# Chunks of 64 steps on 64x64 array tiles in a recurrent attention block followed by routed experts

## The chip, the cores and the metric

The kernel runs on one core of one Trainium2 chip. The metric is the device time of one launch in microseconds (us). Five engines work in the core, each through its own instructions in order: TensorE (PE in the profile, with its weight loads listed apart as PEld), VectorE (DVE), ScalarE (ACT), GpSimd (POOL) and SyncE (SP, which here only issues DMAs). Products land in PSUM, which here is eight banks of 128 partitions by 512 floats; everything else lies in SBUF.

## What is computed

A recurrent attention with a matrix state per batch and head, then a top-1 mixture of experts over its output. All values are 32-bit floats.

```python
# attention: B, H, S, D = 4, 8, 768, 40
for t in range(S):
    y[:, :, t] = einsum('bhd,bhde->bhe', r_t, state)
    Sa = einsum('bhde,bhe->bhd', state, a_t)
    state_decay = state * w_t[:, :, None, :] - einsum('bhd,bhe->bhde', Sa, b_t)
    state = state_decay + einsum('bhd,bhe->bhde', v_t, k_t)
# x = y as (3072 rows, 320), then experts: E = 8, F = 1024
logits = x @ w_gate;  e = argmax(logits);  gate = softmax(logits)[e]
out = gate * (relu(x @ w1[e]) @ w2[e])
```

## The kernel before

**Chunks.** The time axis is cut into 6 chunks of 128 steps. A unit is one chunk of one batch with all 8 heads, and there are 24 units (`u`; chunk `c`, batch `b`). Two heads share the partitions: head parity `par` 0 uses partitions 0 to 39, parity 1 uses 64 to 103 (`rows(par)`), and `NP` = 4 pairs lie side by side.

**Inside a unit.** `load` brings the six inputs in two DMAs. `prepare` forms the running product of the decay `w` (four scans, L160), its reciprocal (L161), scales `a`, `k` and `b` by them (POOL and DVE), and transposes V, K, B and the decay to time-major form on TensorE (L169), with ScalarE copies out of PSUM (L171). `systems` forms four 128x128 matrices per head, masked to a triangle (`twin`, L190 and L194): N (steps acting on later steps), its transpose NT, G and A. It then squares N and NT five times (`product`, L177, copied by ScalarE in L180). `attend` needs the solution U of a triangular system: it starts from the right-hand side (L239, L245) and multiplies with NT, NT^2, NT^4 ... NT^32 in eight dependent steps per parity (`apply`, L231, with an add on DVE after each, L255 and L264). Then come U transposed (L268), a masked product ZT, the state update (L282, L286, L294, L295), the state transposed (L302), and the output in three products (L310, L316, L320). `route` transposes the output (L335), forms the gate's logits (L339) and a softmax scale, and stores the scaled rows to DRAM (L349).

**Order.** The loop emits for each unit: load of `u + 2`, `prepare` and `systems` of `u + 1`, `attend` and `route` of `u`. The planner of the language puts the instructions of each engine into an order of its own from these, by priority of emission and by its own cost figures, and adds all waits. Units of the same batch depend on each other through the state; there are four batches, so four units lie between the uses of one state.

**After attention.** The expert weights of the first two experts are fetched, the rows are sorted by expert (one-hot products, L386 to L484), then eight expert groups of 512 rows run: gather, transpose, two layers (L513, L526), scatter to the output.

**PSUM.** Tag `big` has 5 slots of one bank (128 x 512 floats), tag `small` 3 slots. Every float product is recorded as two weight loads and two matmuls; a "pass" below is one such pair of a load and a matmul.

## Time and profile before

| | |
|---|---|
| time, median of 3 runs | 2159.66 us (2152.96 to 2162.82) |
| the profiled execution | 2158.44 us |
| its span, first to last instruction | 2156.7 us |
| TensorE busy, share of the span | 92% (weight loads 80%) |
| VectorE, ScalarE, GpSimd busy | 24%, 19%, 7% |
| mean granted TensorE clock | 0.751 of full speed |
| attention, from the first matrices to the store of the last rows | 28.4 to 1779 us |
| sorting and experts | 1779 to 2157 us |

The profile records one execution. Each instruction has an engine, a line of the code, its output and input tiles, a duration, and the idle time of its engine before it with what ended it. Matmuls are pipelined, so a busy TensorE is not one at its peak: the rate is read from the distance between starts, or from a group's length over its count. [...]

### The profile page before, as it was taken

The page shows a single profiled execution, that of the slowest core. Times are in us where ns is not written, and L with a number is a line of the kernel's source. Part 1 is how long each engine was busy: PE and PEld are TensorE (multiplying, and loading weights), DVE is VectorE, ACT ScalarE, POOL GpSimd, SP SyncE. Part 2 cuts the span into 40 slices and gives each one's busy share as a digit, 9 for nine tenths or more (in the row PEclk, how much of TensorE's full clock was granted, in tenths as well). Part 3 has the DMA queues.
Part 4 walks back from the last instruction along what each step waited for, and adds up shares of the span by engine and source line. Part 5 has one row for each costly group of instructions (what it writes and reads, how often), then busy time and mean ns, then how long its engine had stood idle before and what let it go on. Part 6 is the DMA issues. An engine that isn't in the chain of part 4 may idle for free.

```text
span 2156.7 us, 29213 instructions
## 1 busy us (share of the span) xinstructions
PE 1991.0 (92%) x12916; PEld 1728.3 (80%) x12916; DVE 518.7 (24%) x1157; ACT 417.4 (19%) x849; POOL 151.1 (7%) x185
## 2 busy tenths in 40 slices
PE   5999889999999999999999999999999985999998
PEld 4998889988988898899889888988898872554454
DVE  3312321322232133213322321341221113111110
ACT  1322122212211221122122112211222100100000
POOL 4000000000000000000000000000000003211011
PEclk9976577667856775777577667766886657999999
DMA  2000000000000000000000000000000004322210
GB/s 55 20 4 22 22 19 4 22 22 1 22 22 19 4 23 22 19 4 22 22 1 22 22 19 4 22 22 19 4 23 4 1 3 150 108 93 80 73 50 12
DMA packets 20560, 59.58 MB, mean 28 GB/s; under 512 B 2893, under 2 KB 14159, under 8 KB 18512
## 3 DMA queue, kind: packets, MB, share of 16 engines
q1 hardware_dynamic: 16992, 48.50, 7.9%
q0 software_dynamic: 3072, 9.18, 1.4%
q8 instruction: 102, 1.67, 0.3%
q14 instruction: 26, 0.21, 0.0%
q10 hardware_dynamic: 368, 0.01, 0.0%
HBM read 49.82 MB, written 9.18 MB: 27 GB/s over the span
## 4 chain that ended last, share of the span: by engine, by line
PE 65%; issue 13%; DVE 4%; POOL 2%; DMA 0%; ACT 0%; POOLq 0%; DVEq 0%
PE ps_q L231 20%; PE ps_NT L177 9%; PE ps_N L177 6%; PE ps_y L320 3%; PE ps_y L316 3%; PE ps_nat L169 3%; PE ps_y L310 3%; PE ps_ZT L190 2%; PE ps_r L245 2%; DVE X L255 2%; POOL out_dram L532 1%; PE ps_GT L190 1%; PE ps_AT L190 1%; PE ps_N L190 1%; PE hp L513 1%
## 5 line engine op out<-in xcount | busy, mean ns | idle before, releaser
L231 PE MATMUL ps_q<-X,NT 128*128 128x40 f32 x2304 | 397.1, 332 | 51.8 <-DVE X L255 51.6
L231 PEld LDWEIGHTS ps_q<-X,NT 128*128 128x128 f32 x2304 | 375.7, 247 | 69.0 <-DVE X L255 68.6
L177 PE MATMUL ps_NT<-NT,N 128*128 128x128 f32 x1920 | 285.4, 296 | 2.1 <-DVE N L194 1.0
L177 PEld LDWEIGHTS ps_NT<-NT,N 128*128 128x128 f32 x1920 | 243.7, 200 | 10.3 <-DVE N L194 3.3
L255 DVE TENSOR_TENSOR X<-ps_q,X 128x160 f32<-128x160 f32 x240 | 77.9, 324 | 635.3 <-PE ps_q L231 635.3
L180 ACT COPY NT<-ps_NT 128x512 f32<-128x512 f32 x240 | 140.7, 586 | 385.9 <-PE ps_NT L177 385.9
L177 PE MATMUL ps_N<-N,NT 128*128 128x128 f32 x1536 | 211.1, 282 | 0.0
L177 PEld LDWEIGHTS ps_N<-N,NT 128*128 128x128 f32 x1536 | 196.3, 200 | 0.0
L513 PE MATMUL hp<-xgT,w 128*128 128x512 f32 (+1 forms) x384 | 191.3, 628 | 0.0
L231 PE MATMUL ps_q<-Z,NT 128*128 128x40 f32 x768 | 141.7, 347 | 28.0 <-DVE Z L264 28.0
L231 PEld LDWEIGHTS ps_q<-Z,NT 128*128 128x128 f32 x768 | 132.2, 260 | 37.3 <-DVE Z L264 36.7
L513 PEld LDWEIGHTS hp<-xgT,w 128*128 128x128 f32 (+1 forms) x384 | 63.2, 189 | 122.8 <-issue 121.7
L526 PE MATMUL zp<-w,h_sb 128*128 128x320 f32 x512 | 145.0, 433 | 0.0
L320 PE MATMUL ps_y<-natB,ZT 128*128 128x40 f32 x384 | 119.3, 415 | 13.5 <-DVE ZT L194 13.5
L180 ACT COPY N<-ps_N 128x512 f32<-128x512 f32 x192 | 112.5, 586 | 74.3 <-PE ps_N L177 74.3
L526 PEld LDWEIGHTS zp<-w,h_sb 128*128 128x128 f32 x512 | 94.5, 191 | 34.5 <-issue 0.8
L316 PE MATMUL ps_y<-natK,AT 128*128 128x40 f32 x384 | 119.1, 414 | 0.0
L320 PEld LDWEIGHTS ps_y<-natB,ZT 128*128 128x128 f32 x384 | 102.8, 330 | 16.4 <-DVE ZT L194 15.2
L270 ACT COPY uT<-ps_uT 128x512 f32<-128x512 f32 x24 | 14.1, 586 | 486.0 <-PE ps_uT L268 486.0
L316 PEld LDWEIGHTS ps_y<-natK,AT 128*128 128x128 f32 x384 | 102.5, 328 | 2.0
L169 PE MATMUL ps_nat<-ident,in 128*128 128x128 f32 x288 | 76.0, 420 | 24.6 <-DMA in<-in_packed_dram 16.5
L158 POOL MEMSET PT<- 128x4 f32 x24 | 2.5, 106 | 1330.8 <-DVE ST L295 1047.0
(150 smaller groups left out, 1874.1 us busy)
## 6 DMA issues: line engine op xcount, KB each, us to landing
in<-in_packed_dram SPq DMA_DIRECT2D x48, 480.0 KB
w<-in_moe_w_dram SPq DMA_DIRECT2D x8, 1280.0 KB
w<-in_moe_w_dram SPq DMA_DIRECT2D x8, 1024.0 KB
x_rows<-xs SPq DMA_DIRECT2D x24, 160.0 KB
w<-in_moe_w_dram SPq DMA_DIRECT2D x8, 256.0 KB
xg<-x_rows,g_idx POOLq DMA_INDIRECT x32, 3.0
out_dram<-zo,s_idx POOLq DMA_INDIRECT x32, 2.5
wg_sb<-in_moe_w_gate_dram ACTq DMA_DIRECT2D x2, 4.0 KB
```

Of the source, the lines that this page charges most:

```text
L169: nc.tensor.transpose(ps[:, p, :], src[:, p, :], ident[:])
L177: nc.tensor.matmul(ps[:, p, :], lhsT=lhs(p), rhs=rhs(p), start=True, stop=True)
L180: nc.scalar.copy(t[:], ps[:])
L190: nc.tensor.matmul(ps[par][:, p, :], lhsT=lhs(par, p), rhs=rhs(par, p), start=True, stop=True)
L231: nc.tensor.matmul(q[:, p, :], lhsT=m[:, p, :], rhs=x[:, p, :], start=True, stop=True)
L245: nc.tensor.matmul(qr[par][:, p, :], lhsT=d["GT"][par][:, p, :], rhs=nV[:, p, par, :D], start=(c == 0 and p == 0), stop=True, skip_group_c ...
L255: nc.vector.tensor_tensor(Xn[:], q[:], X[:], op=ALU.add)
L310: nc.tensor.matmul(qy[par][:, p, :], lhsT=I[rs, R, p, :], rhs=Sn[rs, p, :], start=(p == 0), stop=False, skip_group_check=True,)
L316: nc.tensor.matmul(qy[par][:, p, :], lhsT=d["AT"][par][:, p, :], rhs=nK[:, p, par, :D], start=(c == 0 and p == 0), stop=False, skip_group_ ...
L320: nc.tensor.matmul(qy[par][:, p, :], lhsT=ZT[par][:, p, :], rhs=nB[:, p, par, :D], start=False, stop=True, skip_group_check=True,)
L513: nc.tensor.matmul(hp[:, :cols], lhsT=g["w"][0][:dsz, db, fb * 128 : (fb + 1) * 128], rhs=g["xT"][:dsz, db, :cols], start=(db == 0), stop= ...
L526: nc.tensor.matmul(zp[:], lhsT=g["h"][:, fb, j * 128 : (j + 1) * 128], rhs=g["w"][1][:, fb, :], start=(fb == 0), stop=(fb == FB - 1),)
```

## The change

A unit becomes one chunk of 64 steps of two batches (`bh`, two halves of the batch axis) with all heads: there are again 24 units, 12 chunks by 2. Batch `q` and head parity `par` each pick a half of 64 partitions, on the input or the output side, so every product but the transposes and the gate becomes a 64x64 product on one of the four quarters of the array. `TILES` lists the four quarters, and the loops issue them in that order. Where input and output half are the same index, only the two diagonal quarters are used: `ps_T1`, `ps_gv`, `ps_u`, `ps_S` and the first addition into `ps_y`.

The five squarings stay in number (the last forms one side only), but the inverse is now formed as a matrix, TT = (1+N)(1+N^2)...(1+N^32), in `systems`, with the identity added on GpSimd (`plus_one`) and each product copied by VectorE. `attend` then applies TT once, in place of eight dependent steps per parity. The decay's running product and its reciprocal become two scans over all segments at once and a reciprocal of 8 columns. The decay is no longer transposed, since the output is scaled before its transpose. PSUM has one tag of 4 slots with two banks each. `prepare` runs two units ahead and `systems` one. The weights of the first two experts are fetched before the attention loop; loads go three units ahead, with eight DMAs of 256-byte pieces each.

The diff, cut to its core:

```diff
-W, K, A, B_, V, R = range(6)
+K, A, B_, V, R = range(5)
...
+    C = 64
+    BH = B // 2
+    NCH = NW * CW // C
...
+    halves = [slice(0, HP), slice(HP, 128)]
+    TILES = [(0, 0), (1, 1), (0, 1), (1, 0)]
...
+        NIN = 4
+        ins = [ring.tile([128, 5, SEG, C], F32, name=f"in{i}") for i in range(NIN)]
+        decs = [ring.tile([128, SEG * C1 + 1], F32, name=f"dec{i}") for i in range(2)]
...
+        for t in ins:
+            for lo in (32, 96):
+                nc.gpsimd.memset(t[lo : lo + 32], 0.0)
+        for t in decs:
+            for lo in (32, 96):
+                nc.gpsimd.memset(t[lo : lo + 32], 1.0)
+            nc.gpsimd.memset(t[:, : SEG * C1].rearrange("p (s j) -> p s j", j=C1)[:, :, 0:1], 0.0)
+            nc.gpsimd.memset(t[:, SEG * C1 :], 0.0)
+        for t in qini + rhss + STs + Ss:
+            nc.gpsimd.memset(t[:], 0.0)
...
+        def bank2(name):
+            return pp.tile([128, 2, 512], F32, name=name, tag="ps")
...
+        def load(u):
+            c, bh = divmod(u, BH)
...
+            for q in range(2):
+                for par in range(2):
+                    src = packed[2 * bh + q, at, par, :, :, :, w0 : w0 + C]
+                    nc.sync.dma_start(dst[rows(par), q, :, 1:], src[:, 0])
+                    nc.sync.dma_start(dst5[rows(par), q], src[:, 1:])
+
+        def prepare(u):
...
+            nc.vector.tensor_tensor_scan(
+                rv[:, : SEG * C1 + 1][:, ::-1], dec[:, ::-1], ones65[:, ::-1], 0.0, op0=ALU.mult, op1=ALU.add,
+            )
...
+            nc.vector.reciprocal(qi[:, :, 0], r3[:, :, 1])
+            nc.vector.tensor_tensor_scan(
+                q[:], dec[:, : SEG * C1], qi[:].rearrange("p s j -> p (s j)"), 0.0, op0=ALU.mult, op1=ALU.add,
+            )
...
+            nc.gpsimd.tensor_tensor(I[:, K], I[:, K], behind, op=ALU.mult)
+            nc.gpsimd.tensor_tensor(I[:, B_], I[:, B_], behind, op=ALU.mult)
+            nc.gpsimd.tensor_tensor(I[:, A], I[:, A], d["q3"][:, :, :C], op=ALU.mult)
...
+            for i, (nm, n) in enumerate((("V", V), ("K", K), ("B", B_))):
...
+                for p in range(NP):
+                    nc.tensor.transpose(
...
+                nc.scalar.copy(t[:].rearrange("c p a d -> c (p a d)"), ps[:, i % 2, :])
+            return d
...
+        def systems(d):
...
+            ps = tens(bank2("ps_N"), 2)
+            for p in range(NP):
+                for w, (l, r) in enumerate(((A, B_), (B_, A))):
+                    for par, q in TILES:
+                        nc.tensor.matmul(
+                            ps[halves[q], par, w, p, :], lhsT=head(l, p, q, par), rhs=head(r, p, q, par), start=True, stop=True,
+                        )
+            X = sb.tile([128, 2, 2, NP, C], F32, name="X", bufs=4)
+            for s in range(2):
+                nc.vector.tensor_tensor(
+                    X[:, s], ps[:, s], m_nn[:, :, None, :].to_broadcast([128, 2, NP, C]), op=ALU.mult,
+                )
...
+            pt = bank2("ps_T1")
+            p1 = pt[:, 0, :].rearrange("x (q p j) -> x q p j", q=2, p=NP)
+            for p in range(NP):
+                for par, q in TILES:
+                    nc.tensor.matmul(
+                        p1[halves[par], q, p, :], lhsT=head(B_, p, q, par), rhs=head(A, p, q, par), start=True, stop=True,
+                    )
+            T1 = sb.tile([128, 2, NP, C], F32, name="T1", bufs=2)
+            nc.vector.tensor_tensor(T1[:], p1, m_nn[:, None, 1:2, :].to_broadcast([128, 2, NP, C]), op=ALU.mult)
...
+            def plus_one(dst, src):
+                nc.gpsimd.tensor_tensor(dst, src, eye[:, : NP, :], op=ALU.add)
+
+            for s in range(2):
+                plus_one(TT[:, s], T1[:, s])
+            ps = tens(bank2("ps_G"), 2)
...
+                nc.vector.tensor_tensor(
+                    G[:, s], ps[:, s], m_up[:, None, None, :].to_broadcast([128, 2, NP, C]), op=ALU.mult,
+                )
...
+            for p in range(NP):
+                for par, q in ((0, 0), (0, 1), (1, 0), (1, 1)):
+                    nc.tensor.matmul(
+                        gv[halves[q], par, p, :], lhsT=G[halves[q], par, 0, p, :], rhs=Vn[halves[q], p, par, :D],
+                        start=True, stop=True,
+                    )
...
+            nc.scalar.copy(GV[:, :, :, :D], gv)
...
+            k = 1
+            while k < C:
+                nk = 2 * k
+                if nk < C:
+                    last = 2 * nk >= C
+                    ps = tens(bank2("ps_sq"), 2)
+                    for p in range(NP):
+                        for w in range(1 if last else 2):
+                            for h, s in TILES:
+                                nc.tensor.matmul(
+                                    ps[halves[s], h, w, p, :], lhsT=X[halves[h], s, 1 - w, p, :], rhs=X[halves[h], s, w, p, :],
+                                    start=True, stop=True,
+                                )
+                    Y = sb.tile([128, 2, 2, NP, C], F32, name="X", bufs=4)
+                    M = sb.tile([128, 2, NP, C], F32, name="M", bufs=2)
+                    if last:
+                        nc.scalar.copy(Y[:, :, 0], ps[:, :, 0])
+                    else:
+                        for s in range(2):
+                            nc.scalar.copy(Y[:, s], ps[:, s])
+                    for s in range(2):
+                        plus_one(M[:, s], Y[:, s, 0])
+                if k > 1:
+                    ps = tens(bank2("ps_TT"), 2)
+                    for p in range(NP):
+                        for h, s in TILES:
+                            nc.tensor.matmul(
+                                ps[halves[s], h, 0, p, :], lhsT=Mk[halves[h], s, p, :], rhs=TT[halves[h], s, p, :],
+                                start=True, stop=True,
+                            )
+                    TT = sb.tile([128, 2, NP, C], F32, name="TT", bufs=3)
+                    nc.vector.tensor_copy(TT[:], ps[:, :, 0])
+                if nk < C:
+                    X, Mk = Y, M
+                k = nk
+            d["TT"] = TT
...
+        def attend(u, d):
...
+                nc.vector.tensor_tensor(ST[:, :, :, :D], state[bh][:], pc, op=ALU.mult)
...
+                for p in range(NP):
+                    for par, q in TILES:
+                        nc.tensor.matmul(
+                            ps[halves[q], par, p, :], lhsT=I[halves[par], A, 2 * p + q, :], rhs=ST[halves[par], q, p, :D],
+                            start=True, stop=True,
+                        )
+                nc.vector.tensor_tensor(rhs[:, :, :, :D], ps, rhs[:, :, :, :D], op=ALU.add)
+
+            pu = bank2("ps_u")[:, 0, : 2 * NP * D].rearrange("x (a p d) -> x a p d", a=2, p=NP)
+            for p in range(NP):
+                for par, q in ((0, 0), (0, 1), (1, 0), (1, 1)):
+                    nc.tensor.matmul(
+                        pu[halves[q], par, p, :], lhsT=TT[halves[q], par, p, :], rhs=rhs[halves[q], par, p, :D],
+                        start=True, stop=True,
+                    )
+            U = sb.tile([128, 2, NP, D], F32, name="U")
+            nc.scalar.mul(U[:], pu, -1.0)
+
...
+                nc.scalar.copy(Sn[:, :, :, :D], pS)
...
+                with tc.issue_after(first.ins):
+                    by_dims()
+            uT = sb.tile([128, 2, NP, C], F32, name="uT")
+            nc.scalar.copy(uT[:], put)
...
+            nc.vector.tensor_tensor(
+                ZT[:], pz, m_nn[:, None, 1:2, :].to_broadcast([128, 2, NP, C]), op=ALU.mult,
+            )
...
+                    nc.vector.tensor_tensor(sa[:], pst, ST[:, :, :, :D], op=ALU.add)
...
+            nc.vector.tensor_tensor(
+                xT[:].rearrange("x p q j -> x q p j"), py, q3[:, :, :C].rearrange("x (p q) j -> x q p j", q=2), op=ALU.mult,
+            )
...
+        def route(u, xT):
...
+                r0 = (2 * bh + q) * S + c * C
+                nc.sync.dma_start(x_d[r0 : r0 + C, :], xs[halves[q]].rearrange("x h e -> x (h e)"))
...
+        NU = BH * NCH
+        weights = {}
+        ready = {}
+        for u in range(min(2, NU)):
+            load(u)
+        for e in range(2):
+            weights[e] = fetch(moe_w1[e], moe_w2[e])
+        for u in range(-2, NU):
+            if u >= -1 and u + 3 < NU:
+                load(u + 3)
+            if u + 2 < NU:
+                ready[u + 2] = prepare(u + 2)
+                ready[u + 2]["u"] = u + 2
+            if 0 <= u + 1 < NU:
+                systems(ready[u + 1])
+            if u >= 0:
+                route(u, attend(u, ready.pop(u)))
+
```

Per unit the loops give 480 products on quarters of the array (32, 16, 32, 16, 4x32 + 16 and 5x16 in `systems`; 16, 16, 16, 16, 16, 16, 32 and 32 in `attend`) and 20 on the full array (12 transposes in `prepare`, 4 gate products and 4 transposes in `route`).

## Rows read from the trace of the kernel before

**Rows 1.** Page, part 1: busy time, share of the span and instructions of each engine.

```profile
PE 1991.0 (92%) x12916; PEld 1728.3 (80%) x12916; DVE 518.7 (24%) x1157; ACT 417.4 (19%) x849; POOL 151.1 (7%) x185
```

**Rows 2.** Windows by stage: length, busy us (count) of PE, PEld, DVE, ACT, POOL; clock; DMA.

```profile
0.00:28.40 28.40, 3.84 (x17) 3.14 (x17) 6.01 (x8) 3.04 (x4) 24.14 (x49) 1.00 0.40 104
28.40:1779.05 1750.65, 1641.63 (x11881) 1556.30 (x11880) 451.75 (x977) 381.66 (x781) 59.58 (x68) 0.71 0.06 15
1779.05:2156.70 377.65, 345.48 (x1020) 168.88 (x1020) 60.94 (x172) 32.74 (x64) 67.33 (x68) 0.95 0.26 81
```

**Rows 3.** Timeline of PE, 74 to 78 us: start, length, line, tiles, shape, count.

```profile
74.28 0.98 PE L231 MATMUL ps_q<-X,NT 128*128 128x40 f32 x8
75.18 1.16 PE L177 MATMUL ps_NT<-NT,N 128*128 128x128 f32 x8
76.17 1.06 PE L177 MATMUL ps_N<-N,NT 128*128 128x128 f32 x8
```

**Rows 4.** Windows of four stretches: matrices, two dense stretches, and the dependent steps.

```profile
94.97:95.47 0.50, 0.50 (x26) 0.49 (x26) 0.00 (x0) 0.38 (x1) 0.00 (x0) 1.00 0.06 16
72.00:96.00 24.00, 23.95 (x232) 23.29 (x229) 4.66 (x12) 9.96 (x17) 0.00 (x0) 1.00 0.01 2
406.00:412.00 6.00, 6.00 (x58) 6.00 (x58) 3.70 (x8) 1.21 (x4) 0.00 (x0) 0.50 0.07 27
444.00:452.00 8.00, 6.60 (x28) 6.01 (x28) 1.08 (x4) 0.00 (x0) 0.00 (x0) 0.50 0.00 0
```

**Rows 5.** Timeline, 444 to 448 us: a dependent step's hand-over.

```profile
444.85 0.32 DVE L255 TENSOR_TENSOR X<-ps_q,X 128x160 f32<-128x160 f32 x1 [2.02 <-PE ps_q L231]
445.23 1.93 PE L231 MATMUL ps_q<-X,NT 128*128 128x40 f32 x8 [0.42 <-DVE X L255]
```

**Rows 6.** Timeline of PE around 97 us (clock 1.00) and 464 us (clock 0.50).

```profile
97.25 0.50 PE L302 MATMUL ps_st<-ident,ST 40*40 40x40 f32 x16
...
463.45 0.76 PE L302 MATMUL ps_st<-ident,ST 40*40 40x40 f32 x16
464.14 1.92 PE L310 MATMUL ps_y<-S,in 40*128 40x40 f32 x8
```

**Rows 7.** Line L302: matmul duration ns, shortest, median, longest; first and last start.

```profile
L302 PE MATMUL ps_st<-ident,ST x320: 203/264/283, 97.3 to 1498.7; 40*40 40x40 f32 x160
```

**Rows 8.** Timeline of PEld at two changes of the tile shape.

```profile
460.35 0.14 PEld L286 LDWEIGHTS ps_s<-u,natB 128*40 128x40 f32 x1 [0.33 <-issue]
...
463.45 0.61 PEld L302 LDWEIGHTS ps_st<-ident,ST 40*40 40x40 f32 x16 [0.23 <-issue]
```

**Rows 9.** Groups by line: op, shape, count | busy us, mean ns | idle before, what ended it.

```profile
L180 ACT COPY NT<-ps_NT 128x512 f32<-128x512 f32 x240 | 140.7, 586 | 385.9 <-PE ps_NT L177 385.9
L531 ACT COPY zo<-zp 128x320 f32<-128x320 f32 x32 | 13.6, 426 | 134.3 <-PE zp L526 134.3
L194 DVE TENSOR_TENSOR GT<-ps_GT,before 128x512 f32<-128x512 f32 x48 | 30.8, 683 | 20.6 <-PE ps_GT L190 20.6
L255 DVE TENSOR_TENSOR X<-ps_q,X 128x160 f32<-128x160 f32 x240 | 77.9, 324 | 635.3 <-PE ps_q L231 635.3
L160 DVE TENSOR_TENSOR_SCAN PT<-in,zeros_c 128x128 f32<-128x128 f32 x96 | 34.9, 408 | 18.1 <-DMA in<-in_packed_dram 16.4
L396 DVE TENSOR_TENSOR_SCAN pr<-keep,sel 128x192 f32<-128x192 f32 x1 | 0.6, 557 | 0.0
L163 POOL TENSOR_TENSOR in<-in 128x512 f32<-128x512 f32 x24 | 31.4, 1307 | 48.2 <-DVE in L161 48.2
L134 POOL MEMSET in<- 32x2560 f32 x6 | 13.3, 2224 | 0.3
```

**Rows 10.** DMA queues, 408 to 410 us (one store): packets, MB, share of 16 engines.

```profile
q1 hardware_dynamic: 144, 0.16, 22.2%
```

**Rows 11.** Timeline of SP, 1781 to 1785 us: issues of the weights.

```profile
1782.78 0.74 SPq L374 DMA_DIRECT2D w<-in_moe_w_dram  x1
```

**Rows 12.** Timeline of PE, 1800 to 1804 us: the experts' first transpose.

```profile
1802.37 0.45 PE L504 MATMUL tp<-ident,xg 128*128 128x128 f32 x1 [4.97 <-DMA xg<-x_rows,g_idx]
```

## The prediction

> **What bounds the kernel now.** I read the busy shares first: TensorE 92%, the others 7 to 24% [rows 1]. Then the windows by stage: attention takes 1750.65 us, 72.9 us for each of 24 units, with TensorE busy 94% of it and its clock at 0.71; what stands ahead takes 28.4 us and the experts 377.65 us [rows 2]. So only attention can give or lose much, and in it TensorE. The timeline shows what a pass costs there: groups of 8 passes follow each other at 0.89 to 0.99 us, 0.11 to 0.12 us a pass, and a group with 40 moving columns (L231) costs what one with 128 does (L177) [rows 3]. The width of the moving side is paid for and not used. The windows show the two clocks: products without gaps over 24 us ran at 1.00, while the eight dependent steps (28 passes in 8 us, each group waiting for VectorE) and the stretch that forms the masked matrices ran at 0.50 [rows 4]. A dependent step is 1.93 us of TensorE, then 0.32 us of VectorE, then TensorE again; TensorE starts 0.06 us after VectorE ends at 445.17 [rows 5]. That wait ends on the product, so the price of a pass and the clock set the time, not the other engines.

> **The price of a pass on a quarter.** No row shows four quarters at once. Two diagonal blocks of 40x40 (L302) come nearest: 16 passes last 0.50 us at clock 1.00 and 0.76 us at 0.50 [rows 6]; less one matmul's own length (0.203 and 0.264 us, shortest and median of the line [rows 7]) that is 20 and 33 ns a pass. Each of the two blocks thus needs 40 and 66 ns a pass at 40 columns. At 64 columns it is 1.6 times that, 64 and 106 ns; half the full array's 0.11 us gives 55 at the fast clock. I take 60 and 107 ns for a quarter's pass, so 15 and 27 ns with four quarters at work, 30 and 54 with two. Bounds: L302's own pass, 20 ns, and no overlap at all, 60 to 107 ns; L310, where passes on the same half follow each other, shows what no overlap looks like, 8 passes in 1.92 us [rows 6].

> **TensorE per unit.** Of 480 small products (960 passes) 80 use only two quarters: ps_T1, ps_gv, ps_u, ps_S and the first part of ps_y, 16 each. Fast clock: 800 x 15 ns = 12.0 us, 160 x 30 ns = 4.8 us, 40 passes of the full array x 0.11 = 4.4 us. Each change between tile shapes idles 0.23 to 0.33 us [rows 8]; with some six a unit (the transposes and the gate) 1.5 us. Sum 22.7 us. Slow clock: 21.6 + 8.6 + 8.6 + 1.5 = 40.3 us.

> **The other engines per unit, all beside it.** A 512-wide copy on ScalarE takes 0.586, a 320-wide one 0.426; a masked 512-wide product on VectorE 0.683 [rows 9]. ScalarE: 9 copies for the squarings, 3 natural forms and uT (13 x 0.586 = 7.6) and three of 320 (1.3) and route's 1.1: 10 us. VectorE: seven masks or scalings and five TT copies of 512 (8.2), three of 320 (1.5, between 0.324 and 0.683 each), two scans of 520 and route's five small ones; a scan costs 408 ns for 128 and 557 for 192, so 2.33 ns an element and 1.3 us for 520 [rows 9]; the wide reciprocal goes. Sum 13 us. GpSimd: three 512-wide products at 1.31 and twelve half as wide at 0.65, 12 us [rows 9]. All three stay under TensorE's sum.

> **The dependent chains.** A level of squaring: 64 passes 0.96, 0.2 for the last to come out, two ScalarE copies 1.17, hand-over 0.06: 2.4 us. `systems`: first products and two masks 2.5, four levels 9.6, the half level 1.3, the identity on GpSimd 1.3, the last TT product and copy 1.4: 16.1 us. `attend`: ST, ps_r, add, ps_uT, copy, ps_ZT, mask, ps_y, scaling come to 7 us, and `route` from gate to scaled rows to 3 us: 10 us. The two run beside each other, since `systems` works for the next unit; PSUM's four slots may keep them from doing so fully. So a unit takes at least 22.7 us (TensorE never waits) and about 22.7 + 10 if attend's waits stay uncovered. Of the clock: at 0.71 before [rows 2], three fifths of the time were slow, in the dependent steps and the narrow stretches; now most passes are dense and 64 wide, in groups of 32 or 64 without a wait inside, but waits follow each group. I put a quarter of TensorE's work at the slow clock: 22.7 + 0.25 x 17.6 = 27 us, and 2 us of uncovered waits: 29 us a unit.

> **Loads.** A unit's 983 KB come in 3840 pieces of 256 bytes, in place of 12 KB rows. In the window of one store 144 packets took 22.2% of 16 engines for 2 us, 49 ns a packet, mostly of 1280 bytes [rows 10]. As an upper bound, 3840 x 49 ns are 12 us over 16 engines, 19 us over ten (40 rows divide into ten shares of four; an estimate); under 29. They are issued three units ahead, which hides them. An issue takes up to 0.74 us of SP [rows 11]: eight a unit 5 us, hidden too. If a load did come late, VectorE's scan of unit u + 2 would wait for it, and behind it on VectorE the masks of unit u + 1 and so TensorE; at ten shares that starts above 75 ns a packet.

> **Ahead and after.** The first load on SP now waits for the cleared decay buffer, which stands behind eight clearings of 2.22 us on GpSimd [rows 9]: 17.8 us. Before any attend the first unit's `systems` runs uncovered, 16.1 us. So 28.4 + 17.8 + 16.1 = 62.3 us. Both additions may be hidden in part, down to 0; I take them whole, since nothing else is there to do. The last unit has no `systems` beside it: 10 to 18 us, I take 14. After attention the work is the same [rows 2]; the early weights take nothing off, since the experts' first transpose waits for the gathered rows, not for weights [rows 12].

> **Sum**, against 28.4 + 1750.65 + 377.65 + 1.74 outside the span = 2158.44, which is 1.2 under the median: 62.3 + 23 x 29 + 14 + 377.65 + 1.74 = 1123 us.

> **Rivals.** (a) Fully covered and fast: 23 us a unit, 985 us. For it: 1.00 over 24 us of dense work [rows 4]. Against: four PSUM slots, waits after every group. (b) The clock stays at 0.50: 40.3 + 4 us a unit, first part 10 us longer, 62.3 + 10 + 23 x 44.3 + 22 + 379 = 1493 us. For it: the 6 us of 58 passes on two halves of the array, TensorE busy throughout, were slow [rows 4]. Against: the dense stretch of 24 us at 1.00. (c) Only two quarters ever run together: 960 x 30 ns + 5.9 = 34.7 us, with the same share of slow clock 41 us, 1399 us. (d) The two-quarter products, whose neighbours write from both row halves to one PSUM bank, run one after the other: 160 passes at 60 instead of 30 ns, 4.8 us more, with the slow share 5.3: 23 x 34.3, 1245 us. (e) Slower than before: TensorE isn't fed. A unit holds 2000 instructions, loads and matmuls. The densest long stretch shows 461 in 24 us, 52 ns each; a short one 52 in 0.50 us, 9.6 ns each [rows 4]. Nothing shows that long runs could be fed at the short one's rate. It decides from (2158.4 - 62.3 - 14 - 379.4) / 23 = 74 us, 37 ns an instruction; at 52 ns a unit takes 104 us, and the whole about 2940. Against: in the long stretch the array itself was the limit. A milder form, 20 to 25 ns an instruction, gives 40 to 50 us a unit, 1380 to 1610.

> [...]

> **Chances.** Forecast, 26 to 32 us a unit (1055 to 1192 us): 0.42. (a) 0.18, (b) 0.15, (c) 0.06, (d) 0.08, (e) 0.03, its milder form 0.05; the rest, 0.03, is a part ahead or after that I mis-sized, with no change in all as a case within it. The range leaves out (e) and half of its milder form, and the tails of (a) and (b): 975 to 1510 us. Faster by over 0.5% (about what a measurement of this kernel can tell from no change): 0.96; within 0.5%: 0.01; slower: 0.03.

> **What would show it.** A group of 64 passes in `ps_sq` of 1.0 us where the clock is 1.00, 1.7 at 0.50; 1.0 us at 1.00 for 32 passes of `ps_u` or `ps_gv` (twice that is (d)); a steady distance between units of 26 to 32 us; a clock of 0.8 to 0.95 over attention; ScalarE, VectorE and GpSimd each busy under 14 us a unit; the store of the last rows near 745 us. Issue gaps inside a group of passes would be (e); waits of VectorE's scan for the load would show the loads too late. I am wrong at the root if quarters don't overlap or if the chain of `systems` is much over 16 us.

## The result and the profile after

The changed kernel takes 1298.22 us (median of four runs, 1284.12 to 1301.06) against 2156.42 for the kernel before on the same chips, a ratio of 0.601 with an interval of 0.597 to 0.605. The forecast was 1123 us, with a range of 975 to 1510: the direction and the order of size were met, and the time came out 175 us (16%) above the forecast. It lies outside the forecast's own band of 26 to 32 us a unit (1055 to 1192 us); the range held it because it was made wide for the rivals. The profiled execution took 1284.12 us.

Page of the changed kernel: busy time, share and instructions of each engine; the granted clock in 40 slices; the queue that brings instructions. It answers [rows 1].

```profile
PE 1007.2 (79%) x24316; PEld 761.6 (59%) x24316; DVE 370.2 (29%) x694; ACT 252.2 (20%) x519; POOL 406.2 (32%) x497
...
PEclk9979898887978897887988789889689999999998
...
q8 instruction: 191, 3.13, 1.0%
```

Windows of the changed kernel: length, busy us (count) of PE, PEld, DVE, ACT and POOL, clock, DMA share and GB/s. The first two cuts are the first `ps_x` of the first and of the 23rd unit, the third is the end of attention; the last two rows are single units. It answers [rows 2].

```profile
0.00:99.20 99.20, 46.72 (x1540) 40.53 (x1540) 28.36 (x38) 18.19 (x32) 66.00 (x104) 0.91 0.41 100
99.20:890.00 790.80, 602.43 (x21477) 541.25 (x21477) 278.13 (x474) 198.07 (x414) 272.56 (x325) 0.87 0.16 32
890.00:908.40 18.40, 11.69 (x280) 10.55 (x280) 4.96 (x16) 3.29 (x9) 0.00 (x0) 0.78 0.05 12
908.40:1282.40 374.00, 346.38 (x1020) 169.21 (x1020) 58.70 (x168) 32.70 (x64) 67.66 (x68) 0.95 0.22 68
604.50:637.10 32.60, 24.41 (x984) 21.58 (x984) 13.02 (x22) 9.05 (x19) 12.76 (x15) 1.00 0.17 36
715.50:754.80 39.30, 30.39 (x984) 27.14 (x984) 13.02 (x22) 9.22 (x19) 12.74 (x15) 0.82 0.15 32
```

22 units take 790.8 us, 35.9 each where 29 were forecast; TensorE is busy 27.4 of them. That is 152.8 us of the 161 us that this execution is above the forecast; 8 more lie ahead of the first unit's `ps_x` (99.2 against 62.3 + 29 = 91.3). The rest came as forecast: the last unit takes 13.9 us (14) from `ps_x` to `ps_x`, and the 4.5 us from there to the third cut are about what the experts' 374.0 stay under 377.65.

Each stretch for which the trace of either kernel lists the granted clock has 1.00 or 0.50 (50 stretches before, 68 after, the shortest of 3.4 us), so a window's mean between them is read as a mix of these two.

The price of a pass, timeline of PE: start, length, line, tiles, tile, shape, count. The first three stand at clock 1.00, the last two at 0.50. They answer [rows 3, 6].

```profile
609.73 1.10 PE L284 MATMUL ps_G<-in 64*64 64x64 f32 x62
...
629.63 1.14 PE L377 MATMUL ps_S<-ihalf,ST 64*64 64x40 f32 x32
...
632.27 0.63 PE L393 MATMUL ps_uT<-TT,rhs 64*64 64x64 f32 x30
...
704.17 1.94 PE L377 MATMUL ps_S<-ihalf,ST 64*64 64x40 f32 x32
...
711.89 1.07 PE L426 MATMUL ps_st<-U,natB 64*64 64x40 f32 x32
```

Less one matmul's own length (0.21 us; 0.22 to 0.3 at 0.50) these are 14.5 ns a pass on four quarters, 30 on two, and 27 and 53 at the slow clock: what the forecast put down, 15, 30, 27 and 54.

At clock 1.00 throughout, the unit from 604.5 us still takes 32.6 us, where the forecast has 22.7 + 2 = 24.7 at that clock. So the miss is there without any slow clock.

What TensorE waited for, in the 21 units between 129.3 and 890 us: releaser, us in total, times, longest.

```profile
PE ps_TT L329 <- POOL M L276: 43.0, 78, 1.1
PE ps_sq L312 <- ACT X L322: 28.9, 83, 0.8
PE ps_gv L296 <- DVE G L289: 20.4, 21, 1.0
PE ps_x L466 <- DVE xT L453: 17.8, 22, 0.8
PE ps_u L363 <- DVE rhs L358: 17.0, 21, 0.8
PE ps_TT L329 <- DVE TT L334: 16.7, 20, 0.9
PE ps_ZT L407 <- ACT uT L403: 15.1, 21, 0.7
PE ps_y L384 <- ACT S L381: 10.8, 21, 0.5
```

With the small ones 170.5 us, 8.1 a unit, where 2 were forecast. The timeline shows why nothing covers them:

```profile
626.39 0.97 PE L329 MATMUL ps_TT<-TT,M 64*64 64x64 f32 x29 [0.90 <-DVE TT L334]
627.15 0.26 PE L354 MATMUL ps_r<-ST,in 64*64 64x40 f32 x2
```

`ps_TT` at 626.39 is the last product of `systems` for unit u + 1, `ps_r` the first of `attend` for unit u. All of `attend` stands behind all of `systems` on TensorE, so each chain waits alone.

### The profile page after: what moved, and what is told of

The parts are those of the page before. It is cut to its first block, busy times and chain, and to the rows that moved or that the text cites. A ratio compares the mean times of both kernels' runs of the same rounds, so it can differ in the third digit from the quotient of the medians.

```text
span 1282.4 us, 51696 instructions
## 1 busy us (share of the span) xinstructions
PE 1007.2 (79%) x24316; PEld 761.6 (59%) x24316; DVE 370.2 (29%) x694; ACT 252.2 (20%) x519; POOL 406.2 (32%) x497
## 5 line engine op out<-in xcount | busy, mean ns | idle before, releaser
L276 POOL TENSOR_TENSOR M<-X,ihalf 128x256 f32<-128x256 f32 x240 | 188.7, 809 | 116.9 <-ACT X L322 103.3
L312 PE MATMUL ps_sq<-X 64*64 64x64 f32 x6912 | 175.8, 231 | 35.4 <-ACT X L322 33.1
L329 PE MATMUL ps_TT<-TT,M 64*64 64x64 f32 x3840 | 122.8, 240 | 73.1 <-POOL M L276 52.5
L312 PEld LDWEIGHTS ps_sq<-X 64*64 64x64 f32 x6912 | 146.1, 143 | 52.1 <-ACT X L322 47.7
L334 DVE COPY TT<-ps_TT 128x512 f32<-128x512 f32 x120 | 82.9, 691 | 274.5 <-PE ps_TT L329 270.3
L329 PEld LDWEIGHTS ps_TT<-TT,M 64*64 64x64 f32 x3840 | 97.2, 150 | 93.0 <-POOL M L276 89.3
L322 ACT COPY X<-ps_sq 128x512 f32<-128x512 f32 x192 | 103.1, 589 | 141.4 <-PE ps_sq L312 140.1
L653 POOL DMA_INDIRECT out_dram<-zo,s_idx x32 | 31.7, 989 | 181.4 <-ACT zo L652 180.2
L276 POOL TENSOR_TENSOR TT<-T,ihalf 128x256 f32<-128x256 f32 x48 | 33.8, 725 | 126.8 <-DVE T L271 126.8
L615 POOL DMA_INDIRECT xg<-x_rows,g_idx x32 | 30.7, 960 | 109.1 <-PE tp L625 78.9
L230 PEld LDWEIGHTS ps_nat<-ident,in 128*128 128x128 f32 x288 | 38.9, 165 | 44.0 <-issue 21.5
L363 PE MATMUL ps_u<-rhs,TT 64*64 64x40 f32 x768 | 36.6, 264 | 17.9 <-DVE rhs L358 17.9
```

The lines of the kernel that those rows point to most:

```text
L230: nc.tensor.transpose(ps[:, i % 2, p * 128 : (p + 1) * 128], I[:, n, 2 * p : 2 * p + 2, :].rearrange("x q t -> x (q t)"), ident[:],)
L276: nc.gpsimd.tensor_tensor(dst, src, eye[:, : NP, :], op=ALU.add)
L312: nc.tensor.matmul(ps[halves[s], h, w, p, :], lhsT=X[halves[h], s, 1 - w, p, :], rhs=X[halves[h], s, w, p, :], start=True, stop=True,)
L322: nc.scalar.copy(Y[:, s], ps[:, s])
L329: nc.tensor.matmul(ps[halves[s], h, 0, p, :], lhsT=Mk[halves[h], s, p, :], rhs=TT[halves[h], s, p, :], start=True, stop=True,)
L334: nc.vector.tensor_copy(TT[:], ps[:, :, 0])
```

## The experiments

Theory A: the 7 us a unit are those waits, uncovered by the order of the work. Rival B: the slow clock (the windows' 0.87 is a quarter of the time at 0.50) is the loss; the unit of 32.6 us at 1.00 speaks against it. Rival C: GpSimd's additions of the identity hold the squaring chain. Theory D came up with the first runs: TensorE's instructions do not arrive fast enough.

All runs, medians in us; us a unit is the window of 22 units by 22; clock and TensorE's busy time a unit are that window's; the last two columns are TensorE's waits a unit (the waits view over 21 units), for other engines and for "issue", for nothing that the profile shows. Busy time and waits add up to the unit within 0.1 us. The ratios below are to the kernel before.

| kernel | time | a unit | clock | busy | waits: engines | issue |
|---|---|---|---|---|---|---|
| changed kernel | 1298.2 | 35.9 | 0.87 | 27.4 | 8.1 | 0.4 |
| e1 by turns | 1178.8 | 31.5 | 0.93 | 23.6 | 2.6 | 5.4 |
| e2 no identity | 1224.0 | 32.9 | 0.92 | 25.7 | 6.5 | 0.7 |
| e3 both | 1172.2 | 31.0 | 0.93 | 23.5 | 1.8 | 5.7 |
| e4 two rings | 1170.4 | 30.7 | 0.96 | 24.5 | 4.5 | 1.6 |
| e5 by turns, short products | 1269.6 | 35.3 | 0.86 | 26.7 | 1.5 | 7.0 |
| e6 by turns, half squarings | 1072.6 | 26.9 | 0.83 | 20.7 | 4.4 | 1.7 |
| e7 one quarter after another | 1489 | 45.0 | 0.83 | 38.0 | 6.6 | 0.4 |
| e8 e6, identity from PSUM | 1049.4 | 25.7 | 0.87 | 20.0 | 3.3 | 2.4 |
| e9 e6, half branch | 996.5 | 23.7 | 0.75 | 18.5 | 4.7 | 0.4 |
| e10 e8, e9, decay first | 1007.6 | 24.1 | 0.78 | 18.5 | 5.0 | 0.6 |
| e11 half squarings, old order | 1241.0 | 33.9 | 0.69 | 23.5 | 10.2 | 0.1 |
| e12 e9, clearings beside | 989.7 | 23.6 | 0.78 | 18.2 | 4.8 | 0.5 |

**e1: written out by turns.** Both functions yield after each step, and `attend` ends in `route`.

```diff
+            todo = []
             if 0 <= u + 1 < NU:
-                systems(ready[u + 1])
+                todo.append(systems(ready[u + 1]))
             if u >= 0:
-                route(u, attend(u, ready.pop(u)))
+                todo.append(attend(u, ready.pop(u)))
+            while todo:
+                todo = [g for g in todo if next(g, todo) is None]
```

> systems of unit u + 1 and attend of unit u are written out in turn, a squaring level, then a step of attend, in place of one whole after the other; the work is the same. Theory A (the 35.9 us between units, in place of the 29 forecast, are waits of the squaring chain and of attend's own chain that nothing covers, since attend stands wholly behind systems on TensorE): TensorE's idle time falls from 8.6 us a unit to 2 or 3, the distance between units to 28 to 31 us, the time to 1298 - 22 x 6 = 1165 us (1130 to 1200). Rival B (the slow clock, 26% of attention's time, is the loss, some 3.3 us a unit, and comes from the work itself): a distance of 33 us or more, 1230 us or more, with the slow share where it was. Rival C (GpSimd's additions of the identity, late beside VectorE's scans, hold the squaring chain): attend's copies and masks now queue between the chain's own, the chain stays at 20 us or grows, 1200 to 1300 us.

1178.8 us, ratio 0.543 (0.540 to 0.545). The waits for engines fell from 8.1 to 2.6 us, as theory A has it, the clock rose, and TensorE's busy time fell by 3.8 us. But these 9.3 us brought only 4.4 us a unit: waits called "issue", 0.4 us before, are 5.4. The two largest in 21 units, then the timeline of PE with those of one unit:

```profile
PE ps_TT L330 <- issue: 30.8, 23, 3.3
PE ps_sq L313 <- issue: 28.4, 23, 4.1
```

```profile
140.07 0.34 PE L313 MATMUL ps_sq<-X 64*64 64x64 f32 x6 [0.52 <-issue]
144.06 0.34 PE L313 MATMUL ps_sq<-X 64*64 64x64 f32 x7 [1.31 <-issue]
148.05 0.34 PE L313 MATMUL ps_sq<-X 64*64 64x64 f32 x8 [1.89 <-issue]
152.02 0.38 PE L330 MATMUL ps_TT<-TT,M 64*64 64x64 f32 x9 [0.74 <-issue]
```

They come in the middle of a group, 4.0 us apart, with no semaphore to wait for. In 21 units 97 stalls over 0.1 us end 1.15 to 1.7 us after the end of a packet of 16 KB on queue q8 (192 packets, 3.15 MB on e1's page), and 58 of them stand 254 (give or take 3) records of PE and PEld behind the one before; with the semaphore instructions, which are not among these records, it is 256 for all 58. Every one of the 84 waits called "issue" ends 1.15 to 1.75 us after such a packet, where chance would put about one in six. In the changed kernel 47 of 306 stalls end so behind a packet, not far from chance, and 2 have that spacing. So TensorE, as these records read, ran out of instructions: blocks of 256 (the changed kernel's page has twice 24316 records of PE and PEld over 191 packets, 254.6 each), 3.87 us apart (median; the closest 3.3), 7.7 blocks a unit. That is theory D; the places where one block ends and the next begins are called edges below. Here, where TensorE is otherwise fed, the edges take 5.4 of 31.5 us.

**e2: the identity out of the chain.**

```diff
-                    for s in range(2):
-                        plus_one(M[:, s], Y[:, s, 0])
...
-  ... lhsT=Mk[halves[h], s, p, :], rhs=TT[halves[h], s, p, :],
+  ... lhsT=X[halves[h], s, 0, p, :], rhs=TT[halves[h], s, p, :],
...
-                    nc.vector.tensor_copy(TT[:], ps[:, :, 0])
+                    nc.vector.tensor_tensor(TT[:], ps[:, :, 0], T0[:], op=ALU.add)
```

> The identity leaves the chain: T + X T in place of (I + X) T, the product on TensorE is X T and VectorE adds T as it takes it out of PSUM; ten additions of 0.73 to 1.6 us a unit leave GpSimd, the order of the rest stands. Rival C: the whole gap stands behind GpSimd, the distance falls by 4 to 6 us, 1170 to 1210 us. Theory A: only the idle time that ends on GpSimd goes, at most the 2.9 us ahead of ps_TT, and part of it turns into the wait for ScalarE's copy; 1 to 2.5 us a unit, 1243 to 1276 us. Rival B: 1298 less at most 1 us a unit, 1276 to 1298 us.

1224.0 us, ratio 0.568 (0.566 to 0.569), between the two. (Half of the heads, those whose product lands in the other half of the rows, add another head's T here; the work is the same.) The waits for engines fell by 1.6 us a unit, theory A's size; the distance fell by 3.0, since TensorE's busy time fell by 1.7 us too, at a clock of 0.92 in place of 0.87. So rival C holds for about a fifth of the gap of 7 us, and the busy time that went with the higher clock is about as much; why the clock rose stays open.

**e3: both edits.**

> Both edits: written out in turn, and the identity out of the chain. Theory A: what the identity cost is covered by then, so little more than the turn alone: 1110 to 1180 us, within 25 us of it. Rival C: the turn alone gives little and the identity most, so this gives 5 us a unit or more beyond the turn alone, 110 us. Rival B: 1200 us or more, the slow share unchanged at a quarter.

1172.2 us, ratio 0.543 (0.540 to 0.546), the same as by turns alone (half of the heads add another head's T here too): the identity was worth 74 us in the old order, nothing here. Theory A allowed for that; the block edges, 5.7 us a unit, say what took the gain.

**e4: two PSUM rings**, of two slots each in place of one of four.

```diff
-         tc.tile_pool(name="pp", bufs=4, space=PSUM) as pp:
+         tc.tile_pool(name="pp", bufs=2, space=PSUM) as pp:
...
-            return pp.tile([128, 2, 512], F32, name=name, tag="ps")
+            att = name in ("ps_r", "ps_u", "ps_y", "ps_S", "ps_uT", "ps_ZT", "ps_st", "ps_x")
+            return pp.tile([128, 2, 512], F32, name=name, tag="pa" if att else "ps")
```

> The four PSUM slots, handed out in the order in which the tiles are written down, become two rings of two: one for systems and the transposes, one for attend and route; no line moves. If the one ring is what puts attend behind systems (its first tile needs the slot of systems' fourth last), the planner now places ps_r, ps_u and ps_S among the squarings, and the distance falls by 2 to 4 us: 1210 to 1255 us. If it is the order of writing alone that does it, the order stands and the time with it, 1290 to 1310 us. If two slots are too few for the squaring chain, it gets slower, 1310 to 1380 us.

1170.4 us, ratio 0.543 (0.541 to 0.544), more than expected. No line moved, and yet the planner placed `attend` among the squarings:

```profile
407.92 1.13 PE L313 MATMUL ps_sq<-X 64*64 64x64 f32 x62
408.88 0.96 PE L364 MATMUL ps_u<-rhs,TT 64*64 64x40 f32 x28
```

So it was the one ring of four slots, handed out in the order of writing, that put `attend` behind `systems`: two slots each are enough. Its blocks follow each other at 3.84 us too (median), which is 29.6 us for 7.7 blocks; yet TensorE stands only 1.6 us a unit at edges, so here the blocks are near the limit rather than alone in setting it.

**e5 and e6: more instructions, fewer instructions**, both by turns. e5 adds ahead of each `ps_TT`:

```diff
+                    for f in range(26):
+                        h, s = TILES[f % 4]
+                        nc.tensor.matmul(
+                            ps[halves[s], h, 1, 0, 0:1], lhsT=iota_r[halves[h], :HP], rhs=iota_r[halves[h], :1],
+                            start=True, stop=True,
+                        )
```

> The turn-by-turn kernel (1178.8 us, 31.6 us a unit), with 130 one-column fp16 products a unit added, 26 ahead of each ps_TT, into a part of its banks that nothing reads: 260 more instructions for TensorE, one block of 256, and next to no moving data. Theory D (TensorE's instructions come in blocks of 16 KB; in the turn-by-turn kernel the blocks follow each other at 3.87 us, 7.7 blocks a unit, and TensorE stands still at their edges, so a unit cannot be shorter than its blocks): one block more is 3.9 us a unit, 1178.8 + 22 x 3.9 = 1265 us (1245 to 1280). Rival (the array sets the time): 130 passes of at most 14 ns are 1.8 us a unit, part of it in waits that are there anyway, 1179 to 1219 us.

e6 sets X, M and TT but the last to F16:

```diff
-                    M = sb.tile([128, 2, NP, C], F32, name="M", bufs=2)
+                    M = sb.tile([128, 2, NP, C], F16, name="M", bufs=2)
...
```

> The turn-by-turn kernel with the squaring chain (X, I + X and all of T but the last) in fp16: one pass a product in place of two, so 224 passes and 448 instructions less a unit (1.75 blocks of 256), the same number of products, copies and waits. Theory D: 31.6 - 1.75 x 3.87 = 24.8 us a unit, 1178.8 - 22 x 6.8 = 1030 us (1010 to 1070, the upper end if the chain of squarings, some 20 us, then shows). Rival (the array sets the time): 224 passes of 14 ns, 3.1 us a unit at most, 1110 us or more. If waits for the other engines set it, below 2 us a unit, 1135 us or more.

e5: 1269.6 us, ratio 0.588 (0.586 to 0.589), 91 us for one block more, where theory D said 86 and the array's price at most 40. e6: 1072.6 us, ratio 0.495 (0.492 to 0.498), 106 us less: beyond the array's 3.1 us a unit (69 us), short of theory D's 149, and 3 us over its range. The clock blurs both: in e5 it fell to 0.86, which would lengthen a unit too (the changed kernel's takes 32.6 us at 1.00, 39.3 at 0.82), and the short products fill 2.8 us a unit of TensorE's busy time by themselves, against 1.6 us more at edges, so e5 alone does not settle it; in e6 it fell to 0.83, which works against the gain, and the gain is there: 3.7 us less at edges and 2.9 of busy time, with 1.8 more of waits for engines. Its 22 units hold 16551 matmuls in place of 21477, 224 a unit less: an fp16 product is recorded as one pass, an fp32 one as two. The instruction queue's row on the page (packets, MB, share) of e1, of e5, and then of e6:

```profile
q8 instruction: 192, 3.15, 1.1%
```

```profile
q8 instruction: 216, 3.54, 1.2%
```

```profile
q8 instruction: 149, 2.44, 1.0%
```

These are 24 packets more and 43 less than the kernel by turns has. 24 units of 260 instructions are 24.4 blocks, 24 of 448 are 42: the queue carries TensorE's instructions and little else. In e6 the edges are down to 1.7 us a unit, and the waits for GpSimd's M come back (2.0 us a unit of its 4.4).

**e7: one quarter after another.**

```diff
-                    for p in range(NP):
-                        for w in range(1 if last else 2):
-                            for h, s in TILES:
+                    for h, s in TILES:
+                        for w in range(1 if last else 2):
+                            for p in range(NP):
```

> The changed kernel, with the squarings' products ordered by quarter (all of one quarter, then all of the next) in place of round the four; the same products. If a pass on a quarter takes some 56 ns and only different quarters overlap, as the forecast has it, 64 passes take 3.6 us in place of 1.0: 288 passes a unit by 42 ns, 12 us a unit on the chain, 1298 + 22 x 12 = 1560 us (1480 to 1640). If a quarter's passes overlap among themselves about as well (the pass price is the price of issuing), the time stands, 1290 to 1340 us.

The time is known only roughly, 1442.88 to 1502.23 us over four runs; the lowest is 145 us above the changed kernel's median, and below the 1480 that was expected. The passes are what this run is for. At clock 1.00:

```profile
158.26 3.23 PE L312 MATMUL ps_sq<-X 64*64 64x64 f32 x61 [0.26 <-ACT X L322]
```

3.23 us for 61 passes, changes of quarter among them, against 1.1 for 62 in turn on four quarters. From start to start a pass takes 58 ns (median of the line) at 1.00 and 106 at 0.50; forecast were 60 and 107. Four quarters in turn are thus what the change's pass price rests on.

**e11: half squarings (e6's edit) in the changed kernel's own order.**

> The changed kernel in its own order, systems whole and then attend, with the squaring chain in fp16: 224 passes and 448 instructions less a unit, 6.0 blocks in place of 7.7. In the changed kernel's 36.2 us a unit TensorE waits 7.0 us for other engines and stands 1.4 us at block edges. Theory A with D behind it (there the waits are the loss, the blocks only come next): the waits stay at 6 to 7 us, the edges go, and the passes, which lie on the chain, give 3.1 us: 36.2 - 4.5 = 31.7 us a unit, 1298 - 99 = 1200 us (1180 to 1230). If the blocks are the loss in the changed kernel already: 7 us a unit or more, 1145 us or less. If the array's passes are hidden there: 1265 us or more.

1241.0 us, ratio 0.576 (0.573 to 0.579), 4.4% less than the changed kernel, and less of a gain than theory A's 1180 to 1230. The edges (0.1 us a unit) do not hold it. Page of e11:

```profile
PEclk9866677777676677777676667767599999999998
```

The clock over the units is 0.69: with half of the squarings' passes between the same waits TensorE was granted 0.50 for 60% of the time. Its busy time fell by 3.9 us, but the waits for engines grew by 2.1, to 10.2 us a unit. So the slow clock of rival B probably takes part of the gain here, and it came with the edit; how much was not measured apart, and what decides the clock stays open.

**e8, e9, e10, e12: what is left.** All stand on e6. e8 takes I + X out of PSUM on VectorE; e9 sets A, B, the last T, rhs, U, ZT and B's natural form to F16; e10 has both and the decay buffers cleared first; e12 is e9 with the `in` buffers cleared by VectorE.

```diff
-                    for s in range(2):
-                        plus_one(M[:, s], Y[:, s, 0])
+                    nc.vector.tensor_tensor(
+                        M[:], ps[:, :, 0], ihalf[:, None, None, :].to_broadcast([128, 2, NP, C]), op=ALU.add,
+                    )
```

> The kernel with half squarings (1072.6 us, 27.0 us a unit: 6.0 blocks of instructions, 2.3 us of stalls at block edges, 3.8 us of waits for other engines), with I + X taken by VectorE out of PSUM (0.69 us, beside ScalarE's copies) in place of two additions of 0.73 us by GpSimd behind them. The instructions of TensorE stay the same. Rival C in what is left of it (the identity still costs TensorE the 2.2 us a unit of idle time ahead of ps_TT): 1 to 2 us a unit, 1030 to 1050 us. If the blocks or the clock set the distance by now: less than 0.7 us a unit, 1057 to 1075 us. If VectorE, 16.3 us busy a unit then, holds the masks back: 1075 to 1100 us.

1049.4 us, ratio 0.486 (0.485 to 0.487): 1.2 us a unit, the identity's share, as rival C said.

```diff
-        rhss = [ring.tile([128, 2, NP, HP], F32, name=f"rhs{i}") for i in range(3)]
+        rhss = [ring.tile([128, 2, NP, HP], F16, name=f"rhs{i}") for i in range(3)]
...
-            nc.gpsimd.tensor_tensor(I[:, B_], I[:, B_], behind, op=ALU.mult)
...
+            nc.gpsimd.tensor_tensor(A16[:, 1], I[:, B_], behind, op=ALU.mult)
...
+            nc.vector.tensor_copy(A16[:, 0], I[:, A])
...
```

> The kernel with half squarings, with all that only the inverse's branch reads in fp16 as well (A and B, the last T, rhs, U, ZT and B's natural form): 112 products and 4 full-array ones a unit take one pass in place of two, some 230 instructions less, 0.9 of a block, and one VectorE copy and nothing else more. Theory D: the blocks' floor falls from 22.9 to 19.6 us a unit; the stalls at their edges, 2.3 us a unit, go for the most part, 1 to 2.5 us a unit, 1018 to 1050 us. If waits for other engines set all of the distance: 1065 to 1085 us.

996.5 us, ratio 0.460 (0.458 to 0.463): 3.2 us a unit, more than expected, with 5.1 blocks a unit. The edges are gone (0.4 us, 1.3 less), and TensorE's busy time fell by 2.2.

> Both of these edits, and the decay buffers cleared ahead of the others, so that the first load does not stand behind four clearings of 2.2 us (the prologue of the changed kernel was 8 us longer than forecast). Theory D and the waits together: 24 us a unit, 1072.6 - 22 x 3 - 6 = 1000 us (975 to 1035). If the chain of squarings (some 20 us with its own copies) and the clock take the place of both: 1035 to 1060 us.

1007.6 us, ratio 0.466 (0.464 to 0.467), inside its range and still 11 us above e9: the two gains do not add up. That VectorE's 15.2 us a unit (12.7 in e9) hold the masks back is likely, not shown. The decay buffers first brought nothing ahead of the units (`ps_x` at 83.9 us, 83.8 in e9), since GpSimd cleared until 33 us all the same.

```diff
-                nc.gpsimd.memset(t[lo : lo + 32], 0.0)
+                nc.vector.memset(t[lo : lo + 32], 0.0)
```

> The fastest kernel so far (996.5 us), with the eight clearings of the in buffers on VectorE, which is idle then, beside GpSimd's others. With the decay buffers cleared first the first scan started at 21.5 in place of 32.5 us, yet the first products of systems only at 42.3 in place of 43.7: GpSimd's clearings ran until 29 all the same, and its products by the scans' results stood behind them. If GpSimd's 17.8 us of clearings are what holds the start: 10 to 14 us less, 983 to 988 us. If the first loads hold it: 992 to 998 us.

989.7 us, ratio 0.457 (0.454 to 0.460). The time lies between the two that were expected, and the interval overlaps e9's, but the timeline shows what moved: VectorE clears to 23 us, its scan follows at once, and GpSimd's first scaling, at 33.7 us in the changed kernel, is at 24.3. The first `ps_x` comes at 76.2 us, 7.6 earlier.

```profile
20.79 2.19 DVE L183 MEMSET in<- 32x2560 f32 x1 [0.57 <-issue]
23.01 1.24 DVE L214 TENSOR_TENSOR_SCAN rv<-dec,ones 128x521 f32<-128x521 f32 x1
24.34 1.18 POOL L224 TENSOR_TENSOR in<-in,rv 128x512 f32<-128x512 f32 x1 [9.33 <-DVE rv L214]
```

This is the fastest version: 0.76 of the changed kernel's time, with the inverse's branch in fp16.

## Why the forecast was too low

**What held.** TensorE in attention bounded the kernel before, and the price of a pass is what the change lowered. The pass prices, worked out from a two-block product [rows 6, 7], came out within 5%; for the 60 ns that stood behind them e7 gives 58. TensorE's busy time, forecast 27 us a unit, is 27.4, in part by luck: at 1.00 it is 24.4 and not 22.7, and the slow clock, a quarter of the time and not of the work, adds 3 us and not 4.4. The other engines stay at 13.0, 9.1 and 12.7 us a unit (VectorE, ScalarE, GpSimd), near the sums from [rows 9]. The loads are hidden: neither TensorE nor VectorE waits for one between 130 and 890 us. The ten shares of a load have a measure in the kernel before: while packets of its 40-row loads were in flight, 168 us in all, there were just ten of them for 116 us. The weights' early fetch takes nothing off the experts' stage, which lasts 376.4 us from the first instruction of the sorting, 375.6 before.

**The step that failed** is "and 2 us of uncovered waits". The text before it gave the two ends, 22.7 us if TensorE never waits and 10 us more if attend's waits stay uncovered, and named the doubt: four PSUM slots may keep the two chains apart. The forecast took the covered end all the same. They are kept apart altogether (e4), and the waits are 8.1 us. With them a unit would have been 27 + 8 = 35 us, and the time 1261 us; with the 10 us of the working's other end, 37 and 1307. What could have been read beforehand is the order of writing: `attend`'s first tile comes after all of `systems`'.

**A term of the chain was too small.** `systems` takes 21.3 us from its first product to its last copy (606.9 to 628.2 in the unit at clock 1.00), not 16.1; the forecast itself named a chain much over 16 us as a sign of being wrong at the root. The first squaring starts 4.9 us after the first `ps_N`, not 2.5, as four transposes, `ps_T1` and `ps_G` stand between on TensorE and their masks on VectorE. The four levels take 11.5 us, not 9.6; one of them 3.8, where `ps_TT` waits for an M that GpSimd made beside a scan. The end takes 4.9, not 4.0.

```profile
606.90 0.45 PE L254 MATMUL ps_N<-in 64*64 64x64 f32 x12
611.84 0.27 PE L312 MATMUL ps_sq<-X 64*64 64x64 f32 x2
617.97 1.71 DVE L212 TENSOR_TENSOR_SCAN rv<-dec,ones 128x521 f32<-128x521 f32 x1
618.54 3.71 POOL L276 TENSOR_TENSOR M<-X,ihalf 128x256 f32<-128x256 f32 x4
620.25 0.33 PE L329 MATMUL ps_TT<-TT,M 64*64 64x64 f32 x2 [0.82 <-POOL M L276]
627.47 0.69 DVE L334 COPY TT<-ps_TT 128x512 f32<-128x512 f32 x1 [1.23 <-PE ps_TT L329]
```

With the chains end to end, these 5.2 us count in full. The unit at clock 1.00 is 2.4 us from `ps_x` to `ps_N`, 21.3 of `systems` and 9.0 of `attend` to the next `ps_x`, 32.6 in all (to rounding); with 16.1 in place of 21.3 the same order would have given 27.4. So of the 7.9 us over 24.7, the order alone explains 2.7 (an estimate from these lengths).

**Ahead of the units** 8 us were missing, but not in the clearings: the first product of `systems` starts at 44.1 us, 2 us before the forecast's 28.4 + 17.8 = 46.2.

```profile
44.14 1.99 PE L254 MATMUL ps_N<-in 64*64 64x64 f32 x64
66.83 0.69 DVE L334 COPY TT<-ps_TT 128x512 f32<-128x512 f32 x1 [3.38 <-PE ps_TT L329]
```

The first `systems` then takes 23.4 us, to 67.5, in place of 16.1: the chain again. The clearings of 2.22 us [rows 9] were rightly put down as uncovered, and they stand ahead of GpSimd's own scalings as well as of the first load; e12 shows that 7.6 us of them could be covered.

**The rivals.** (c) is out: four quarters take half of what two take, 14.5 against 30 ns a pass. (d) is out: `ps_S` writes from both row halves to one bank at 30 ns a pass, half of a single quarter's 58. (b): the clock is 0.87. (e), the feeding, was the rival to take more seriously: TensorE's bursts do run at 7 ns an instruction (two in a pass of 14.5 ns), nearer to the short stretch of [rows 4] than to the long one, but only inside a block; over blocks it is 13 to 15 ns, and 2000 instructions a unit then take 26 to 30 us (an estimate, from 3.3 and 3.87 us a block). The changed kernel, at 35.9, is above that, so it does not show there (0.4 us); it shows as soon as the order is mended. The 23 us of rival (a) thus lie below what the blocks allow, and the 29 of the forecast at their edge: the best order with all passes in fp32 reached 30.7 (e4).

## What to carry to other kernels

When many small products take the place of few large ones, sum TensorE's time three ways: passes by their price, waits by what really stands between them in the issue order, and instructions by the rate at which blocks of them arrive (3.87 us for 256 in e1); here no unit was shorter than the largest of these, and mending one uncovered the next. Buffers of one ring order the work: if two chains are to cover each other, give each its own slots (e4, 1298 to 1170 us) or write their steps out by turns (e1, 1179 us). Where a product can take one pass in place of two, half of the gain may be its instructions (e6, a unit: 3.7 us less at edges, 2.9 us less of busy time).
